# Attention and gated convolution on one core: x transposed by the DMA crossbar, exp written in token order, attention one step earlier

## The chip, the cores and the metric

The kernel runs on one core of a Trainium2 chip. The time is that of the device, in microseconds (us), from one launch; every kernel was timed several times on the same chip as the kernel before, in turn. A run counts as slow when it is more than 1.5% above the fastest of its kernel, and only fast runs enter a ratio. Engines are named as the profile has them: PE (TensorE matmul), PEld (weight load), DVE (VectorE), ACT (ScalarE), POOL (GpSimd), SP (SyncE, whose queue issues most stores and SBUF-to-SBUF transfers). PEclk is the TensorE clock that was granted, as a share of the full one.

## The reference, cut to what matters

Eight batches of eight heads, 576 tokens, head size 64. Keys and values are averaged over groups of eight tokens, so each head attends to 72 keys. The result x (576 x 512 a batch) goes through a feed-forward layer with a three-tap convolution along the tokens.

```
scores = q @ mean8(k).T / 8;  x = softmax(scores) @ mean8(v)      # per head
h   = relu(x @ w_in)                                              # 512 -> 1024
c   = conv_w[0]*h[t-1] + conv_w[1]*h[t] + conv_w[2]*h[t+1]        # along tokens
out = (h * sigmoid(c)) @ w_out                                    # 1024 -> 512
```

## The kernel before

One batch is 72 score columns a head on 72 partitions, then x with tokens on partitions, then xT with channels on partitions, because `mm1` contracts over channels. PSUM is four slots of two banks, shared by everything that PE writes; PE stops when no slot is free. A batch's loop has eight steps, each one `mm1` (eight matmuls) with a piece of the convolution, of `mm2` (an output tile) or of the next batch's attention between. Variable names: `sc_ps` scores, `attnT` their exp, `av_ps` attention times values, `h_ps` `mm1`, `c_ps` convolution, `o_ps` `mm2`, `kdup` the end of the key tree (three DVE additions that average the keys).

The scores of a head come out in the order (two, i, g), where token = 36 g + 2 i + two. Before, exp wrote rows of 16 adjacent elements in the kernel's own order, and the transpose of x put the tokens right without an instruction of its own, by a permuted identity and the copy out of PSUM:

```
def scores(b, h):
    ...                                         # two matmuls into ps[0:72, two, 0:288]
    nc.scalar.activation(
        out=at.rearrange("s (i two g) -> s two i g", two=2, g=QG),
        in_=ps[0:Sp, :, 0:SC].rearrange("s two (i g) -> s two i g", g=QG),
        func=ACT.Exp, scale=1.0 / (POOL * 8.0))

def xt(b, tiles):                               # PE transposes, 4 for each of 5 tiles
    ...
    nc.tensor.transpose(out=y[:, pr, :, ...], in_=st[b]["x"][i][...], identity=perm)
    ...
    nc.vector.tensor_copy(out=st[b]["xT"]...[:, :, :, r0:r0 + w - skip], in_=y[...])

def batch(b):                                   # cut: steps 4 to 7 of eight
    mm1(b, order[4]); conv(b, 0, 0); att[4](); pool_keys(b + 2); gate(b, 0, 0)
    mm1(b, order[5]); conv(b, 0, 1); att[5](); gate(b, 0, 1)     # att[5]: av 0, 1
    mm1(b, order[6]); tile_out(); ...; att[6](); att[7]()        # av 2-4; xt 0, 1
    mm1(b, order[7]); att[8](); tile_out()                       # xt 2-4
```

`pool_keys(n)` is the key tree of batch n, followed by the load of the keys of n + 1 into the buffer that the tree has just freed.

The softmax here doesn't subtract the row's maximum and nothing guards it: scores larger than these inputs give would overflow.

## Time and profile before

| | before |
|---|---|
| time, median of 3 runs | 250.67 us (248.53 to 253.44) |
| span of the profiled run | 245.7 us |
| steady batch (five loads of q, four intervals) | 26.5 us |
| PE transposes of x in a batch | 20, some 1.3 us of PE |
| exp | 64, 655 ns each |

The page of the profile of before. The first line is the busy time of each engine, with its share of the span and its instructions; the next two the chain of waits that ended last, by engine and by line; the others are groups of instructions (line, engine, operation, what it writes and reads, shapes, count | busy us, mean ns of one | idle time just before them and what ended it).

```profile
PE 218.3 (89%) x3153; PEld 142.7 (58%) x3153; DVE 156.9 (64%) x287; ACT 121.3 (49%) x209; POOL 30.9 (13%) x58
...
PE 62%; ACT 15%; DVE 11%; DMA 5%; issue 5%; POOL 0%; DVEq 0%; SPq 0%; ACTq 0%; POOLq 0%
PE o_ps L304 25%; PE h_ps L238 22%; ACT attnT L181 5%; PE q_ps L160 4%; PE c_ps L272 4%; ACT tg L281 4%; DVE x L205 3%; DVE o L314 3%; DMA qr<-in_q_dram 3%; DMA hT_108<-hT_108 3%; ACT hT_108 L246 3%; ACT hT_109 L246 2%; PE xt_ps L221 2%; PE kT_ps L148 1%; ACT o L312 1%
...
L238 PE MATMUL h_ps<-xT,w_in_sb 128*128 128x288 bf16 x512 | 77.3, 298 | 5.1 <-DVE xT L228 2.3
...
L181 ACT ACTIVATE attnT<-sc_ps 72x576 bf16<-72x576 f32 x64 | 37.2, 655 | 19.1 <-PE sc_ps L173 19.1
...
L221 PE MATMUL xt_ps<-perm,x 128*128 128x128 bf16 x160 | 15.1, 236 | 5.9 <-DVE x L205 3.9
```

PE is busy 89% of the span and makes up 62% of the chain. Exp takes 655 ns for 576 elements. The Trainium skill, "ScalarE: Activation LUTs", section "What ACT_TABLE_LOAD costs", gives 186 ns + 0.833 ns an element, which would be 666 ns: the trace agrees. The transposes' 15.1 us of PE are pipelined; eight of them move the chain by 0.52 us.

One line of before: the instructions that write the tile `perm` (count: least/median/most ns, first and last start).

```profile
L351 DVE COPY perm<-ident x1: 445/445/445, 6.0 to 6.0; 128x128 bf16<-128x128 bf16 x1
```

It is the only copy of before whose neighbouring writes lie far apart, 16 bytes here; memsets are left aside.

### The profile page before, as it was taken

How to read it: one execution, taken by the hardware profiler on the slowest of the kernel's cores; microseconds unless marked ns; L12 is line 12 of the kernel's file. 1: busy time of each engine (PE TensorE's matmuls, PEld its weight loads, DVE VectorE, ACT ScalarE, POOL GpSimd, SP SyncE). 2: the span in 40 equal slices, each digit the busy share in tenths (PEclk: the TensorE clock that was granted, in tenths of full speed). 3: DMA queues.
4: the chain of work that ended last, by engine and by line, in shares of the span. 5: the costliest groups of instructions: out<-in, count | busy, mean ns of one | idle time of the engine just before them, and what ended most of it. 6: DMA issues, size and time to landing. Idle time of an engine off the chain costs nothing.

```text
span 245.7 us, 7301 instructions
## 1 busy us (share of the span) xinstructions
PE 218.3 (89%) x3153; PEld 142.7 (58%) x3153; DVE 156.9 (64%) x287; ACT 121.3 (49%) x209; POOL 30.9 (13%) x58
## 2 busy tenths in 40 slices
PE   0487998559999999999999999999999999999993
PEld 0455665337666756666566665675666666656441
DVE  5678448683858585668684877668594826553341
ACT  2070379112681659236843586255925693267510
POOL 5442364010200011000200020001000000000000
PEclk9999999756999999999999999999999999999998
DMA  5999899969896288926895589628832223133323
GB/s 82 165 140 135 164 173 219 202 86 142 191 178 153 78 175 128 241 84 120 152 188 137 105 160 186 169 80 177 151 108 69 91 69 95 75 113 95 124 88 128
DMA packets 29908, 33.26 MB, mean 135 GB/s; under 512 B 5788, under 2 KB 24244, under 8 KB 29876
## 3 DMA queue, kind: packets, MB, share of 16 engines
q0 software_dynamic: 16976, 16.27, 45.0%
q1 hardware_dynamic: 12900, 16.54, 20.9%
q8 instruction: 24, 0.39, 0.6%
q14 instruction: 8, 0.07, 0.1%
HBM read 32.52 MB, written 9.44 MB: 171 GB/s over the span
## 4 chain that ended last, share of the span: by engine, by line
PE 62%; ACT 15%; DVE 11%; DMA 5%; issue 5%; POOL 0%; DVEq 0%; SPq 0%; ACTq 0%; POOLq 0%
PE o_ps L304 25%; PE h_ps L238 22%; ACT attnT L181 5%; PE q_ps L160 4%; PE c_ps L272 4%; ACT tg L281 4%; DVE x L205 3%; DVE o L314 3%; DMA qr<-in_q_dram 3%; DMA hT_108<-hT_108 3%; ACT hT_108 L246 3%; ACT hT_109 L246 2%; PE xt_ps L221 2%; PE kT_ps L148 1%; ACT o L312 1%
## 5 line engine op out<-in xcount | busy, mean ns | idle before, releaser
L238 PE MATMUL h_ps<-xT,w_in_sb 128*128 128x288 bf16 x512 | 77.3, 298 | 5.1 <-DVE xT L228 2.3
L304 PE MATMUL o_ps<-w_out_sb,gT 128*128 128x512 bf16 x288 | 67.1, 379 | 0.8 <-DVE gT L291 0.8
L238 PEld LDWEIGHTS <-w_in_sb 128*128 128x128 bf16 x512 | 50.6, 101 | 25.3 <-issue 7.9
L181 ACT ACTIVATE attnT<-sc_ps 72x576 bf16<-72x576 f32 x64 | 37.2, 655 | 19.1 <-PE sc_ps L173 19.1
L304 PEld LDWEIGHTS <-gT 128*128 128x128 bf16 x288 | 27.8, 98 | 29.5 <-DVE gT L291 1.3
L246 ACT ACTIVATE hT_109<-h_ps 128x576 bf16<-128x576 f32 x32 | 21.0, 656 | 44.5 <-PE h_ps L238 44.5
L281 ACT ACTIVATE tg<-c_ps 128x576 bf16<-128x576 f32 x64 | 38.4, 664 | 0.6 <-PE c_ps L272 0.6
L246 ACT ACTIVATE hT_108<-h_ps 128x576 bf16<-128x576 f32 x32 | 21.0, 657 | 24.9 <-PE h_ps L238 24.9
L205 DVE TENSOR_TENSOR x<-av_ps,r 128x512 bf16<-128x512 f32 x40 | 27.7, 692 | 1.4
L314 DVE COPY o<-o_ps 128x512 f32<-128x512 f32 x20 | 13.8, 692 | 18.2 <-PE o_ps L304 18.2
L312 ACT COPY o<-o_ps 128x512 f32<-128x512 f32 x16 | 9.4, 586 | 29.5 <-PE o_ps L304 29.5
L272 PEld LDWEIGHTS <-dw 32*32 32x32 bf16 x1536 | 14.1, 88 | 11.5 <-issue 8.0
L221 PE MATMUL xt_ps<-perm,x 128*128 128x128 bf16 x160 | 15.1, 236 | 5.9 <-DVE x L205 3.9
L221 PEld LDWEIGHTS <-x 128*128 128x128 bf16 x160 | 11.5, 104 | 8.6 <-DVE x L205 7.0
L194 PEld LDWEIGHTS <-attnT 72*128 72x128 bf16 x320 | 13.3, 102 | 4.3 <-ACT attnT L181 0.9
L113 POOL DMA_DIRECT2D qr<-in_q_dram x8 | 4.9, 617 | 81.9 <-PE q_ps L160 79.9
L165 DVE COPY qT<-q_ps 128x1152 bf16<-128x1152 bf16 x16 | 12.1, 756 | 4.8 <-PE q_ps L160 4.5
L173 PE MATMUL sc_ps<-qT,kz_104 128*72 128x288 bf16 x64 | 12.2, 326 | 1.2 <-DVE qT L165 0.8
L160 PE MATMUL q_ps<-ident,qr 128*128 128x128 bf16 x144 | 12.5, 243 | 0.7 <-DMA qr<-in_q_dram 0.7
L204 DVE RECIPROCAL r<-av_ps 128x8 f32<-128x8 f32 x40 | 8.0, 201 | 7.4 <-PE av_ps L194 7.4
L272 PE MATMUL c_ps<-hT_108,dw 32*32 32x288 bf16 x768 | 12.0, 287 | 0.8 <-ACT hT_108 L246 0.5
L228 DVE COPY xT<-xt_ps 128x1024 bf16<-128x1024 bf16 (+1 forms) x24 | 12.0, 548 | 0.1
(163 smaller groups left out, 188.8 us busy)
## 6 DMA issues: line engine op xcount, KB each, us to landing
out_dram<-o SPq DMA_DIRECT2D x36, 256.0 KB, 2.6
qr<-in_q_dram POOLq DMA_DIRECT2D x8, 576.0 KB, 6.2
kr<-in_k_dram POOLq DMA_DIRECT2D x7, 576.0 KB, 11.8
vr<-in_v_dram POOLq DMA_DIRECT2D x7, 576.0 KB, 10.8
hT_108<-hT_108 SPq DMA_DIRECT2D x16, 108.0 KB, 4.6
hT_109<-hT_109 SPq DMA_DIRECT2D x16, 108.0 KB, 4.0
hT_108<-hT_108 SPq DMA_DIRECT2D x16, 72.0 KB, 3.9
hT_109<-hT_109 SPq DMA_DIRECT2D x16, 72.0 KB, 2.2
```

What stands on the lines that cost most here:

```text
L160: nc.tensor.transpose(out=ps[:, i * P:(i + 1) * P], in_=st[b]["q"][:, i0 + i, :], identity=ident)
L173: nc.tensor.matmul(out=ps[0:Sp, c2, 0:SC], lhsT=kz[b % 2][:, h, c2, :], rhs=st[b]["qT"][:, h].rearrange("d i g -> d (i g)"), start=True, s ...
L181: nc.scalar.activation(out=at.rearrange("s (i two g) -> s two i g", two=2, g=QG), in_=ps[0:Sp, :, 0:SC].rearrange("s two (i g) -> s two i ...
L194: nc.tensor.matmul(out=ps[:, h // 4, c:c + D + 1], lhsT=st[b]["at"][h][:, t0:t0 + P], rhs=va[b % 2][:, h, :], start=True, stop=True,)
L205: nc.vector.tensor_tensor(out=x.rearrange("p (g h) d -> p g h d", g=2), in0=y[:, :, :, 0:D], in1=r.unsqueeze(3).to_broadcast([P, 2, 4, D]) ...
L221: nc.tensor.transpose(out=y[:, pr, :, ii * RT:(ii + 1) * RT], in_=st[b]["x"][i][:, 2 * pr:2 * pr + 2, :].rearrange("p h d -> p (h d)"), id ...
L238: nc.tensor.matmul(out=ps[:, c, 0:SC], lhsT=w_in_sb[:, dc, fb * P:(fb + 1) * P], rhs=xT[:, dc, c * SC:(c + 1) * SC], start=(dc == 0), stop ...
L246: nc.scalar.activation(out=row[:, PAD:S + PAD].rearrange("p (c n) -> p c n", c=NS), in_=ps[:, :, 0:SC], func=ACT.Relu, scale=0.5,)
L272: nc.tensor.matmul(out=ps[j // 2][QD * c:QD * (c + 1), j % 2, 0:SC], lhsT=dw[QD * r:QD * (r + 1), kk, g * NQ + j, :], rhs=row[QD * r:QD * ...
L281: nc.scalar.activation(out=tg[:, 2 * i:2 * i + 2, :], in_=ps[i][:, :, 0:SC], func=ACT.Tanh)
L304: nc.tensor.matmul(out=ps[:, 0, :], lhsT=gT[:, fb, j * P:(j + 1) * P], rhs=w_out_sb[:, fb, :], start=(fb == 0), stop=(fb == n_fb - 1),)
L314: nc.vector.tensor_copy(out=o, in_=ps[:, 0, :])
```

## The change

Its intent was to take the 140 transposes of batches 1 to 7 off PE and the copies off DVE. The crossbar transpose, as it is issued here, keeps the order of the tokens that it finds, so exp has to write them in token order. Attention moves up by a step to hide the transfers' time.

```diff
-            out=at.rearrange("s (i two g) -> s two i g", two=2, g=QG),
+            out=at.rearrange("s (g i two) -> s two i g", two=2, g=QG),
             in_=ps[0:Sp, :, 0:SC].rearrange("s two (i g) -> s two i g", g=QG),
...
+    def xt_dma(b, i):
+        t0, r0 = i * P, row0[i]
+        nc.sync.dma_start_transpose(
+            out=st[b]["xT"][:, :, t0:t0 + P - r0],
+            in_=st[b]["x"][i][r0:P].rearrange("p h d -> p (h d)"))
...   # xt() keeps PE for batch 0, now with the plain identity
         def a5():
-            av(n, 0)
-            av(n, 1)
+            for i in range(3):
+                av(n, i)
+                xt_dma(n, i)
         def a6():
...                                   # the same for tiles 3 and 4; a7, a8 gone
         mm1(b, order[0])
-        att[0]()
+        att[1]()                      # every att one step earlier
...
         mm1(b, order[4]); conv(b, 0, 0)
-        att[4](); pool_keys(b + 2); gate(b, 0, 0)
+        att[5](); gate(b, 0, 0); pool_keys(b + 2)
...
         mm1(b, order[7])
-        att[8]()
+        st[b + 2]["att"][0]()
         tile_out()
```

In exp only the output's layout changed: the innermost index g, adjacent before, now steps by 36 tokens, 72 bytes.

## The prediction

> **What bounds the kernel.** TensorE. The busy table gives PE 89% of the 245.7 us span, VectorE 64%, ScalarE 49%; the chain of waits is 62% PE, 15% ACT, 11% DVE. In the steady state one batch takes 25.7 or 27.1 us (four or five output tiles; read from the chain). Adding one batch's PE pieces from the chain (8 x 0.97 h_ps, 4.5 x 1.73 o_ps, 4 x 0.66 c_ps, 16 x 0.12 scores, 1.1 q, 0.4 k, 1.3 av, 1.3 xt) gives about 24.2 us, so some 2.2 us a batch are stalls, mostly where ScalarE's evictions (exp, tanh, Relu) free the four PSUM slots too late: the chain goes ACT attnT, hT, tg there.
>
> **Removed.** In seven batches 20 PE transposes each (8 took 0.52 us in the chain: 1.3 us a batch, 9 us in all, nearly all on the critical path), the three VectorE copies to xT (0.68+0.68+0.28 = 1.6 us a batch, mostly off it).
>
> **Added.** Five crossbar transposes a batch on SP's queue. SP now issues some 17 transfers a batch at 0.5-0.6 us. The Trainium skill, "VectorE: DVE Perf Modes", section "The three transpose paths", gives 1309 ns for one 128x128 by crossbar; no trace here shows one. My estimate: 1.2-2.5 us of SP per 128x512 transpose and about 3 us to land. The next batch's first mm1 needs the last two some 5 us after their issue: about covered, 0-1 us of stall a batch.
>
> **exp in token order.** Its innermost writes go from adjacent to 72 bytes apart. The Trainium skill, "Advanced Engine Details and Errata", section "SBUF Cachelines", says that a different 16-byte line for each access costs. The one such write in the trace agrees on VectorE: the perm copy (128 elements, 16 bytes apart) took 445 ns, where the fixed part of its copies is near 155 and one element a cycle would add 133. If ScalarE pays likewise (I say 60%), exp goes from 655 to about 1135 ns, 3.8 us a batch. In steps 1 to 3 (where tanh of two convs, Relu and eight exps now meet) ScalarE then has 14.7 us of work against 11.9 of PE, and PE loses about 2 us a batch there.
>
> **Moved.** Attention a step earlier puts av 0-2, two gates, the key tree (1.22+0.69+0.69), av 3-4, the kz and qT copies into steps 4 to 7: some 12 us of VectorE against 11 of PE. av 3 and 4 hold PSUM slots behind the key tree; I reckon 1.5-2.5 us of PE stall a batch there. That eats the 1.3 us.
>
> **Sum.** Without an exp penalty: about 246 us. With it: about 262 us (7 x 2 us, and some 2 us at the start). Weighted: 256 us, 8 in 10 between 240 and 272. Faster by over 2%: 0.28; within 2%: 0.22; slower: 0.5.
>
> **What would show it.** exp's mean in the groups of instructions (655 or over 1000 ns); the transposes' issue time on SP and their time to landing; in the waits, h_ps waiting for a DMA to xT (transposes late), PE waiting for x of VectorE (key tree in the way), or for attnT of ScalarE (exp slow); a steady batch of 25 us (right without penalty) or 27-28 us.
>
> **What would make it wrong.** ScalarE writing strided at full rate and VectorE keeping up: then 238-242. A transpose that keeps SP over 3 us: the queue then fills, hT turns and outputs come late, and it is over 270.

## The result

The changed kernel takes 363.5 us (median of 4 runs, 361.25 to 364.43) against 250.4 us for before (4 runs, 248.53 to 253.44). The ratio is 1.454, 95% interval 1.442 to 1.466. A ratio here is the mean time of one kernel's fast runs over that of the other's of the same rounds, so it is not quite the ratio of the medians quoted.

The page of the changed kernel, the same lines: busy time, chain, and the group of exp.

```profile
PE 244.8 (67%) x3013; PEld 148.2 (41%) x3013; DVE 145.7 (40%) x265; ACT 244.9 (68%) x209; POOL 30.3 (8%) x58
...
ACT 41%; PE 26%; DVE 12%; issue 10%; DMA 9%; POOL 0%; DVEq 0%; SPq 0%; ACTq 0%; POOLq 0%
ACT attnT L180 35%; PE h_ps L246 11%; PE o_ps L312 7%; DMA xT<-x 7%; DVE x L204 3%; PE c_ps L280 3%; PE q_ps L159 3%; ACT tg L289 2%; DMA qr<-in_q_dram 2%; DVE gT L299 2%; PE av_ps L193 2%; ACT hT_107 L254 1%; DVE r L203 1%; ACT hT_108 L254 1%; DVE kdup L135 1%
...
L180 ACT ACTIVATE attnT<-sc_ps 72x576 bf16<-72x576 f32 x64 | 163.2, 2883 | 11.1 <-PE sc_ps L172 11.1
```

One exp now takes 2883 ns in place of 655. (Records of exps that follow each other overlap. By busy time one exp costs 163.2 / 64 = 2.55 us of ACT against 37.2 / 64 = 0.58.) ACT's busy time has doubled, from 121 to 245 us, and it makes 41% of the chain, where PE had 62%. The list of waits (engine, line, what it waited for: us in total, times, longest) shows where PE lost its time.

```profile
PE sc_ps L172 <- ACT attnT L180: 41.1, 30, 2.1
...
PE av_ps L193 <- ACT attnT L180: 22.2, 12, 2.2
...
PE o_ps L312 <- ACT attnT L180: 11.5, 9, 1.5
...
PE h_ps L246 <- DMA xT<-x: 8.3, 4, 4.7
PE c_ps L280 <- ACT attnT L180: 7.4, 6, 1.6
```

These four waits of PE for exp add up to 82 us (41.1 + 22.2 + 11.5 + 7.4). The timeline shows how: in order of start, start and length in us, instructions merged, in brackets the idle time before.

```profile
182.08 1.12 PE L172 MATMUL sc_ps<-qT,kz_103 128*72 128x288 bf16 x4 [2.06 <-ACT attnT L180]
...
182.37 7.64 ACT L180 ACTIVATE attnT<-sc_ps 72x576 bf16<-72x576 f32 x3
...
187.59 0.40 PE L172 MATMUL sc_ps<-qT,kz_103 128*72 128x288 bf16 x2 [0.42 <-ACT attnT L180]
...
190.06 0.41 PE L172 MATMUL sc_ps<-qT,kz_103 128*72 128x288 bf16 x2 [2.07 <-ACT attnT L180]
```

Three exps take 7.64 us together, the next scores wait for a PSUM slot for up to 2.07 us, and so do convolution and output tiles, which use the same slots. The mean granted clock fell as well, to 0.849 (before 0.969); e12 below shows how a wait brings it down.

The crossbar did what was expected of it on SP's side. The tile xT in the trace (least/median/most ns of one issue; then us from issue to landing):

```profile
L216 SPq DMA_TRANSPOSE xT<-x x35: 1182/1218/2297, 72.7 to 326.8; - x35
...
DMA to landing us min/median/max: 2.3/3.1/7.9
```

A transpose of 128 x 512 elements keeps SP for 1.22 us and lands after 2.3 us at best.

### The profile page after: what moved, and what is told of

The parts are those of the page before. It is cut to its first block, busy times and chain, and to the rows that moved or that the text cites. A ratio compares the mean times of both kernels' runs of the same rounds, so it can differ in the third digit from the quotient of the medians.

```text
span 362.7 us, 7083 instructions
## 1 busy us (share of the span) xinstructions
PE 244.8 (67%) x3013; PEld 148.2 (41%) x3013; DVE 145.7 (40%) x265; ACT 244.9 (68%) x209; POOL 30.3 (8%) x58
## 4 chain that ended last, share of the span: by engine, by line
ACT 41%; PE 26%; DVE 12%; issue 10%; DMA 9%; POOL 0%; DVEq 0%; SPq 0%; ACTq 0%; POOLq 0%
ACT attnT L180 35%; PE h_ps L246 11%; PE o_ps L312 7%; DMA xT<-x 7%; DVE x L204 3%; PE c_ps L280 3%; PE q_ps L159 3%; ACT tg L289 2%; DMA qr<-in_q_dram 2%; DVE gT L299 2%; PE av_ps L193 2%; ACT hT_107 L254 1%; DVE r L203 1%; ACT hT_108 L254 1%; DVE kdup L135 1%
## 5 line engine op out<-in xcount | busy, mean ns | idle before, releaser
L180 ACT ACTIVATE attnT<-sc_ps 72x576 bf16<-72x576 f32 x64 | 163.2, 2883 | 11.1 <-PE sc_ps L172 11.1
L246 PE MATMUL h_ps<-xT,w_in_sb 128*128 128x288 bf16 x512 | 91.8, 334 | 9.7 <-DMA xT<-x 8.3
L312 PE MATMUL o_ps<-w_out_sb,gT 128*128 128x512 bf16 x288 | 71.0, 396 | 12.4 <-ACT attnT L180 11.5
L246 PEld LDWEIGHTS <-w_in_sb 128*128 128x128 bf16 x512 | 56.0, 112 | 36.3 <-DMA xT<-x 9.5
L254 ACT ACTIVATE hT_108<-h_ps 128x576 bf16<-128x576 f32 x32 | 23.9, 746 | 42.1 <-PE h_ps L246 42.1
L254 ACT ACTIVATE hT_107<-h_ps 128x576 bf16<-128x576 f32 x32 | 24.5, 767 | 33.8 <-PE h_ps L246 33.8
L193 PEld LDWEIGHTS <-attnT 72*128 72x128 bf16 x320 | 18.2, 123 | 27.1 <-issue 16.5
L172 PE MATMUL sc_ps<-qT,kz_104 128*72 128x288 bf16 x64 | 14.2, 321 | 22.1 <-ACT attnT L180 21.7
L172 PE MATMUL sc_ps<-qT,kz_103 128*72 128x288 bf16 x64 | 14.4, 341 | 20.6 <-ACT attnT L180 19.4
L280 PEld LDWEIGHTS <-dw 32*32 32x32 bf16 x1536 | 15.8, 91 | 24.5 <-issue 18.2
L193 PE MATMUL av_ps<-va_105,attnT 72*128 72x65 bf16 x160 | 10.5, 232 | 13.7 <-ACT attnT L180 13.5
L172 PEld LDWEIGHTS <-kz_104 128*72 128x72 bf16 x64 | 7.4, 121 | 28.9 <-issue 27.2
L172 PEld LDWEIGHTS <-kz_103 128*72 128x72 bf16 x64 | 8.3, 132 | 26.8 <-issue 22.8
L99 POOL DMA_DIRECT2D kr<-in_k_dram x9 | 7.3, 814 | 136.8 <-DVE t_840 L121 27.2
```

What stands on the lines that cost most here:

```text
L172: nc.tensor.matmul(out=ps[0:Sp, c2, 0:SC], lhsT=kz[b % 2][:, h, c2, :], rhs=st[b]["qT"][:, h].rearrange("d i g -> d (i g)"), start=True, s ...
L180: nc.scalar.activation(out=at.rearrange("s (g i two) -> s two i g", two=2, g=QG), in_=ps[0:Sp, :, 0:SC].rearrange("s two (i g) -> s two i ...
L193: nc.tensor.matmul(out=ps[:, h // 4, c:c + D + 1], lhsT=st[b]["at"][h][:, t0:t0 + P], rhs=va[b % 2][:, h, :], start=True, stop=True,)
L246: nc.tensor.matmul(out=ps[:, c, 0:SC], lhsT=w_in_sb[:, dc, fb * P:(fb + 1) * P], rhs=xT[:, dc, c * SC:(c + 1) * SC], start=(dc == 0), stop ...
L254: nc.scalar.activation(out=row[:, PAD:S + PAD].rearrange("p (c n) -> p c n", c=NS), in_=ps[:, :, 0:SC], func=ACT.Relu, scale=0.5,)
L280: nc.tensor.matmul(out=ps[j // 2][QD * c:QD * (c + 1), j % 2, 0:SC], lhsT=dw[QD * r:QD * (r + 1), kk, g * NQ + j, :], rhs=row[QD * r:QD * ...
```

## The experiments

There is no e10. Before ran too; its median is beside each result.

### Which part of the change costs the time: e1 to e4

**e1_exp_alone**: before, with exp's new write order and a plain identity in the PE transposes, nothing else.

```diff
-            out=at.rearrange("s (i two g) -> s two i g", two=2, g=QG),
+            out=at.rearrange("s (g i two) -> s two i g", two=2, g=QG),
```

> Before, with one part of the change: exp writes in token order (16 writes 72 bytes apart in a row), PE transposes with the plain identity, order of before. Theory W (the exp's write order costs nearly everything): exp near 2.9 us each, and 64 of them add some 143 us of ScalarE work, of which 90 to 120 us show: 340 to 370 us. Rival D (crossbar transposes or the moved attention slow the exp or cost the time): exp near 0.65 us, time within 10 us of before's 250.

372.3 us against 248.8, ratio 1.496, just above the range expected. The group of exp:

```profile
L182 ACT ACTIVATE attnT<-sc_ps 72x576 bf16<-72x576 f32 x64 | 163.9, 2894 | 18.6 <-PE sc_ps L174 18.6
```

Exp is as slow without a single crossbar transpose, and this kernel is slower than the whole change. Rival D falls: the write order alone costs more than the change loses, and the rest of the change wins a little back while ACT is the limit.

**e2_after_adjacent**: the changed kernel with the old, adjacent writes. The token order is then wrong.

```diff
-            out=at.rearrange("s (g i two) -> s two i g", two=2, g=QG),
+            out=at.rearrange("s (i two g) -> s two i g", two=2, g=QG),
```

> The changed kernel, with exp's writes adjacent again as before; crossbar transposes and moved attention stay. Wrong result on purpose (tokens in the kernel's inner order). Theory W: exp 0.65 us, time 240 to 256 us. Rival D: exp stays above 2 us or the time stays above 300 us.

265.8 us against 248.8, ratio 1.054; exp 649 ns. (Two of its four runs were slow; the fast ones took 261.5 and 263.2 us.) Most of the loss is gone, but not all: 265.8 lies between what the two theories said. With these small inputs the attention is nearly uniform; putting q's tokens into the wrong order in the reference itself changes the output by only 0.5% of its norm. So the comparison does not see token order here, and order has to be checked by reading.

**e3_after_i_inner** and **e4_after_two_inner**: the changed kernel, same elements, same places, same values; only the order in which the activation runs over them differs.

```diff
# e3: writes 4 bytes apart, PSUM read 64 bytes apart
-            out=at.rearrange("s (g i two) -> s two i g", two=2, g=QG),
-            in_=ps[0:Sp, :, 0:SC].rearrange("s two (i g) -> s two i g", g=QG),
+            out=at.rearrange("s (g i two) -> s two g i", two=2, g=QG),
+            in_=ps[0:Sp, :, 0:SC].rearrange("s two (i g) -> s two g i", g=QG),
# e4: writes adjacent, PSUM read alternating between two banks
+            out=at.rearrange("s (g i two) -> s g i two", two=2, g=QG),
+            in_=ps[0:Sp, :, 0:SC].rearrange("s two (i g) -> s g i two", g=QG),
```

> The changed kernel; exp computes and writes the same elements to the same places, but runs over i innermost: writes 4 bytes apart, PSUM reads 64 bytes apart. If the cost comes from the step between successive writes: exp 0.65 to 1.0 us, time as with adjacent writes, within 10 us. If it comes from the scattered layout as such, or from reading PSUM with a step as much as from writing: exp stays over 2 us.

> The same with two innermost: writes wholly adjacent, PSUM reads alternate between two banks (2048 bytes apart). If only the write step counts: exp 0.65 to 0.75 us and the fastest of the correct forms. If the read step counts too: slower than with i innermost.

e3 took 266.0 us (262.7 to 266.9, two of four runs slow) and e4 264.6 us, ratio 1.062; the times don't tell the two apart. The group of exp in e3 and in e4:

```profile
L180 ACT ACTIVATE attnT<-sc_ps 72x576 bf16<-72x576 f32 x64 | 45.7, 810 | 15.0 <-PE sc_ps L172 14.9
```

```profile
L180 ACT ACTIVATE attnT<-sc_ps 72x576 bf16<-72x576 f32 x64 | 37.0, 649 | 17.9 <-PE sc_ps L172 17.9
```

So the layout that the change wants costs exp nothing when the activation's innermost run is adjacent in SBUF. Neither of the two read patterns tried slowed it: with PSUM jumps of 2048 bytes between elements exp took 649 ns, and e3's 810 ns with PSUM steps of 64 bytes is what writes 4 bytes apart cost without them (806 ns, e11 below). The change's 363.5 us fall to e4's 264.6 us, 99 us, by an edit of the loop order.

**e5_order_pe**, a control: before with e4's exp order, the plain identity and PE transposes.

> Control: before with exp in token order by two innermost, plain identity, PE transposes, order of before. exp 0.65 us, time within 3 us of before: token order costs nothing when the innermost run is adjacent in SBUF.

250.5 us against 250.6; its profiled run was a slow one, and the ratio of the fast runs is 0.988, interval 0.977 to 0.999, from two fast runs. Token order is free in this kernel.

### How the cost grows with the step: e11

**e11_write_steps**: before with extra exps near the start, from one PSUM slot into a scratch tile, each form three times on its own line.

```diff
+    # k = 1, 2, 3, 4, 6, 8: one element every 2k bytes, never coming back
+    nc.scalar.activation(out=scr[...].rearrange("s (two n k) -> s two n k", two=2, k=k)[:, :, :, 0],
+                         in_=sps[0:Sp, :, 0:SC], func=ACT.Exp, scale=...)
+    # then the change's own form, i inner, two inner, and fp32 adjacent and 144 bytes apart
```

> Before with extra exps near the start into a scratch tile, three of each form: writes 2, 4, 6, 8, 12 and 16 bytes apart (monotone), the 72-byte interleaved form of the change, i innermost, two innermost, and fp32 adjacent and 144 bytes apart. If only the step between successive writes matters: 0.65 us up to some step, and as slow as 2.6 to 3.0 us at 16 bytes and above. If it is the coming back to the same lines that costs: 16 bytes monotone stays under 1.3 us and only the interleaved form is near 2.9.

The time (290 us) is that of before plus the extra work and says nothing. The groups of the scratch writes; L365 to L375 are steps of 2, 4, 6, 8, 12 and 16 bytes, L377 is the change's form, L379 i inner, L381 two inner, L383 fp32 adjacent, L385 fp32 144 bytes apart:

```profile
L375 ACT ACTIVATE scr<-sps 72x576 bf16<-72x576 f32 x3 | 8.1, 2710 | 0.1
...
L377 ACT ACTIVATE scr<-sps 72x576 bf16<-72x576 f32 x3 | 7.9, 2635 | 0.1
...
L373 ACT ACTIVATE scr<-sps 72x576 bf16<-72x576 f32 x3 | 6.2, 2075 | 0.1
...
L371 ACT ACTIVATE scr<-sps 72x576 bf16<-72x576 f32 x3 | 4.3, 1439 | 0.1
...
L385 ACT ACTIVATE scr<-sps 72x576 f32<-72x576 f32 x3 | 3.5, 1171 | 0.1
L369 ACT ACTIVATE scr<-sps 72x576 bf16<-72x576 f32 x3 | 3.4, 1122 | 0.1
...
L367 ACT ACTIVATE scr<-sps 72x576 bf16<-72x576 f32 x3 | 2.4, 806 | 0.1
L379 ACT ACTIVATE scr<-sps 72x576 bf16<-72x576 f32 x3 | 2.4, 804 | 0.1
L365 ACT ACTIVATE scr<-sps 72x576 bf16<-72x576 f32 x3 | 2.0, 650 | 0.1
L381 ACT ACTIVATE scr<-sps 72x576 bf16<-72x576 f32 x3 | 1.9, 647 | 0.1
L383 ACT ACTIVATE scr<-sps 72x576 f32<-72x576 f32 x3 | 1.9, 644 | 0.1
```

The times from 4 to 16 bytes lie on a line: 176 ns + 4.4 ns for each 16 bytes that the writes step through. A step of 4 bytes touches 144 such lines (estimate 810 ns, measured 806), 8 bytes 288 (1443; 1439), 12 bytes 432 (2077; 2075), 16 bytes 576 (2710; 2710). The two constants are fitted to these runs. At 72 bytes it is 2635 ns, no more than at 16, so the cost fits one charge for each 16-byte line entered, and it saturates. Coming back to the same lines (L377) is not what costs, as L375 never does. The Trainium skill, "Advanced Engine Details and Errata", section "SBUF Cachelines", names 16-byte lines and a penalty for a different line at each access; the trace agrees and adds the size. Four-byte elements pay less: 1171 ns at 144 bytes would be (1171 - 176) / 576 = 1.7 ns for each line, an estimate from this one point with the 176 ns of the two-byte line. Why two-byte writes pay 4.4 was not settled.

### What is left, 16 us: the crossbar or the move? e6 and e7

In e4 PE waited for xT and for the key tree:

```profile
PE h_ps L246 <- DMA xT<-x: 18.9, 6, 4.7
PE kT_ps L147 <- DVE kdup L135: 12.4, 3, 7.7
```

**e6_move_alone**: the earlier attention alone; exp, identity and PE transposes as before. The cut is shown against the changed kernel.

```diff
-            for i in range(3):
-                av(n, i)
-                xt_dma(n, i)
+            for i in range(3):
+                av(n, i)
...
+        att[7]()                      # xt 0, 1 by PE
         mm1(b, order[7])
+        att[8]()                      # xt 2 to 4 by PE
```

> The changed kernel's earlier attention alone: exp adjacent and PE transposes through perm, as before (transposes in the same place, end of the batch). Theory L (with exp mended, what is left of the loss is the crossbar transposes' latency at the end of a batch): 246 to 254 us, apart from the wait for kdup at the first handover (PE waited 7.7 to 9.4 us for it in the runs with exp mended), so up to 260. Rival M (the moved attention piles VectorE work up behind the key tree and costs the time): 258 us or more with PE waiting for x or kdup in every batch.

254.0 us against 250.8, ratio 1.011, interval 1.000 to 1.022. The move costs about 1%, and PE's longest listed waits (for `kdup`, 8.4 us) lie at two places only, not in every batch. Rival M falls.

**e7_crossbar_alone**: the crossbar, with e4's exp order, in the order of before.

```diff
         def a5():
             av(n, 0); av(n, 1)
+            xt_dma(n, 0); xt_dma(n, 1)
         def a6():
             av(n, 2); av(n, 3); av(n, 4)
+            xt_dma(n, 2); xt_dma(n, 3); xt_dma(n, 4)
-        def a7(): xt(n, [0, 1])
-        def a8(): xt(n, [2, 3]); xt(n, [4])
```

> Crossbar transposes alone, in the order of before, with exp in token order by two innermost (0.65 us). Theory L: av ends a step later than in the changed kernel, so the first matmuls of each batch wait longer for xT, 3 to 6 us more in each of seven batches: 275 to 300 us. Rival M: with the move undone the loss goes: 245 to 256 us.

276.0 us against 250.8, ratio 1.097. Its wait for xT:

```profile
PE h_ps L248 <- DMA xT<-x: 38.0, 12, 13.1
```

Twice e4's 18.9 us. The crossbar needs the move; with it, it still waits.

### Why the transposes land late: e8, e9, e12, e13, then e14

**e8_late_handover**: e4 with the second batch's key tree put back behind the first `mm1` of batch 1.

```diff
-        pool_keys(2)                  # end of the first batch
-        st[2]["att"][0]()
...
+        else:                         # batch 1, after mm1(b, order[0])
+            pool_keys(2)
+            att[0]()
```

> As e4_after_two_inner, but the second batch's key tree, its k turn and the first half of its q go back behind the first matmul group of batch 1, as before. If that early key tree only moves the wait for the load of k (PE waits for kdup 7.7 us at once): 256 to 262 us against e4's 264.6. If the wait for xT takes its place: no change, 263 to 266.

265.3 us, ratio 1.062, as e4. The wait for `kdup` fell from 12.4 to 6.3 us and that for xT rose from 18.9 to 25.2: the wait for xT took its place, as the second branch said.

**e9_mix**: e8, with tiles 3 and 4 by PE.

```diff
             for i in range(3, 5):
                 av(n, i)
-                xt_dma(n, i)
+        def a7():
+            xt(n, [3, 4])             # after mm1(b, order[7])
```

> As e8_late_handover, but only x tiles 0 to 2 go by crossbar; tiles 3 and 4, which are ready last, by PE. Theory L: the first half of mm1 needs tiles 0 to 2, issued 6 us earlier, so the waits for xT go, 12 of 20 transposes are saved (0.8 us a batch): 242 to 249 us, at or below before. Rival M: 256 us or more.

250.1 us against 250.8, ratio 1.000. The waits for xT went, apart from one of 5.2 us at the first handover, and so did the loss, but there was no gain: PE now waited 7.2 us for x.

**e12_keys_late** and **e13_mix_keys_late**: e8 and e9 with two edits more. Batch 1 is transposed by PE, and the key tree goes behind x tiles 3 and 4 in DVE's queue.

```diff
         att[5]()
         gate(b, 0, 0)
-        pool_keys(b + 2)
...
         att[6]()
         gate(b, 0, 1)
+        pool_keys(b + 2)
```

> Crossbar transposes of all five tiles for batches 2 to 7 (batches 0 and 1 by PE, as the loads crowd the DMA engines there), exp two innermost, and the key tree (2.6 us of VectorE) behind x tiles 3 and 4 instead of ahead of them. Theory L: tiles 3 and 4 are issued 2.6 us earlier, the waits for xT go, PE keeps the 1.3 us a batch: 240 to 247 us. If the last landing still comes too late (waits for xT of 1 us or more a batch): 248 to 256 us.

> The same, but tiles 3 and 4 by PE and only 0 to 2 by crossbar. Saves 0.8 us of PE a batch in six batches: 242 to 249 us, no wait for xT. If it is no faster than before, PE's stalls behind VectorE (x, o) took the saving.

e12 missed both its branches: 267.4 us against 250.6, ratio 1.064. e13: 250.7, ratio 0.992, interval 0.984 to 1.001, no clear gain. The edit hardly did what it was meant to do. At the handover below, x tiles 3 and 4 were ready at 103.4 and 104.2 us, but SP's queue held the first three transposes and two transfers of `hT` until 105.5 us. So the two went out 4.5 us ahead of the next batch's first matmul (105.99 against 110.51), where e8 had 4.1 us (113.78 against 117.89): 0.4 us gained in place of 2.6. So e12 does not test an earlier issue. Its timeline around that handover:

```profile
105.99 2.65 SPq L216 DMA_TRANSPOSE xT<-x  x2
...
106.80 0.80 POOL L99 DMA_DIRECT2D kr<-in_k_dram  x1 [15.32 <-DVE t L121]
...
110.51 0.65 PE L246 MATMUL h_ps<-xT,w_in_sb 128*128 128x288 bf16 x4
...
116.54 1.14 PE L246 MATMUL h_ps<-xT,w_in_sb 128*128 128x288 bf16 x4 [5.38 <-DMA xT<-x]
```

Two transposes are issued from 106.0 us. From 106.8 us POOL issues the load of the next keys, 576 KB, which the key tree has just made room for. The second half of `mm1` needs tiles 2 to 4 and waits 5.38 us, until 116.5. The same stretch by windows of 2 us (length, then busy us and instructions of PE, PEld, DVE, ACT and POOL, granted clock, DMA share, GB/s):

```profile
core 0: us, PE busy (x) PEld busy (x) DVE busy (x) ACT busy (x) POOL busy (x), PEclk, DMA share, GB/s
...
112.00:114.00 2.00, 0.00 (x0) 0.00 (x0) 0.00 (x0) 0.00 (x0) 0.00 (x0) 0.88 0.97 127
114.00:116.00 2.00, 0.00 (x0) 0.00 (x0) 0.00 (x0) 0.00 (x0) 0.00 (x0) 0.50 1.06 83
116.00:118.00 2.00, 1.46 (x36) 0.77 (x37) 0.00 (x0) 0.28 (x1) 0.00 (x0) 0.50 1.02 375
118.00:120.00 2.00, 2.00 (x60) 1.50 (x28) 0.30 (x1) 1.56 (x3) 0.04 (x1) 0.50 0.19 58
120.00:122.00 2.00, 2.00 (x58) 1.30 (x57) 1.97 (x4) 0.91 (x2) 0.55 (x1) 0.91 0.50 67
```

While PE waits, the DMA engines are fully taken (share about 1) at a mere 83 to 127 GB/s. The wait costs twice: the granted clock falls to 0.50 and is back at 0.91 only some four us after work returns. The Trainium skill, "TensorE: Matmul & The Clock Gate", section "Part 1: The HAM clock gate", has the clock halved after an idle window of about 3.4 us, which does not start with the idle time. The trace shows the half, but already some 2.4 us after PE went idle near 111.2 us (in windows of 0.5 us the clock is 1.00 until 113.5 us and 0.54 in the next), sooner than 3.4 us of idling alone would have it; at e12's next long wait, from 144.4 us, it came after some 3.3 us. For the slow transfers the Trainium skill, "DMA: Bandwidth & Descriptors", section "Issuing engines are not separate DMA queues", is the page to have in mind: transfers of all issuing engines run on the same 16 DMA engines and interleave. If so, that SP issues the transposes and POOL the load does not keep them apart; e14 tests it.

**e14_k_load_later**: e12, with the load of the keys moved behind the load of q in POOL's queue. The load of q waits for a PE transpose that comes after the batch's first `mm1`, so the keys now start when xT has arrived.

```diff
-            pool_keys(b + 2)          # key tree, then load_k(b + 3)
+            k_tree(b + 2, 0, H)
...
         att[1]()                      # first step: q, load_q(b + 2)
+        if b > 1 and b + 2 < B:
+            load_k(b + 2, 0, H)
```

> As e12_keys_late, but the next load of k is issued behind the load of q, after a batch's first matmuls, and no longer from the key tree just as transposes 3 and 4 go out. Theory C (what is left of the crossbar's loss is that its last transposes share the DMA engines with the k load): the worst landing falls from 9.0 to about 4 us, PE's waits for xT from 10.5 to under 4 us, time 244 to 254 us. Rival F (the crossbar's own latency is too long for this place): waits and time stay as in e12, 262 to 268 us.

250.0 us against 249.25, ratio 0.994, interval 0.988 to 1.001; e12 had 1.064. That is 17 us by moving one load. PE's list of waits has no wait for xT any more. The profiled runs show the double cost: of 18.6 us less span (263.8 to 245.2), 11.9 are idle time before `mm1` (15.9 to 4.0) and 5.7 are busy time of PE (215.2 to 209.5), whose matmuls had run at the halved clock. The landing times of e14:

```profile
DMA to landing us min/median/max: 2.3/2.9/6.4
```

For e12 and then for e16 below, which also has the moved load, the time that PE waited for xT, how often, and the landing times:

```profile
  DMA xT<-x: 10.5, 4
...
DMA to landing us min/median/max: 2.3/2.5/9.0
```

```profile
  DMA xT<-x: 1.8, 2
...
DMA to landing us min/median/max: 2.3/3.2/6.3
```

Theory C holds and rival F falls: the load is what makes the transposes late. That the two compete for the DMA engines, and not for another part that both use, is read from the engines' share of about 1 alone. The worst landing fell less than expected (to 6.4 us in e14), but the late ones no longer meet a waiting PE.

### A version that beats both, and what makes it: e15 to e18

**e15_mix_k_load_later**: e13 with the moved load.

> As e13_mix_keys_late (tiles 0 to 2 by crossbar, 3 and 4 by PE) with the k load moved the same way. Theory C: little to gain, as no wait for xT was left: 245 to 251 us. A candidate to beat before.

250.6 us, ratio 1.002: no gain from the mix.

**e16_k_load_later_keys_early**: e14 with the key tree ahead of tiles 3 and 4 again, as the change has it.

```diff
         att[5]()
         gate(b, 0, 0)
+        k_tree(b + 2, 0, H)
...
         gate(b, 0, 1)
-        k_tree(b + 2, 0, H)
```

> As e14, but the key tree ahead of x tiles 3 and 4 again, as in the change. Theory C: transposes 3 and 4 go out 2.6 us later, still without the k load beside them: slower than e14 by 0 to 7 us. If as fast: PE's position in the queue, not the key tree, set the end.

244.9 us against 249.25, ratio 0.985, interval 0.979 to 0.991: faster than both kernels, though by less than 2%. Its six runs (241.9 to 246.4 us) lie below the fastest of before (247.25). That it beats e5, the PE transposes with the new exp order (0.988, interval 0.977 to 0.999), is not shown. It is faster than e14, against what was expected of it. PE waited 11.9 us for `kdup` in e14, at seven places, and 6.0 us here, at three: a key tree that is late holds up the next batch's k transposes on PE.

**e17_pe_same_schedule**: e16 with all transposes by PE (the only edit is the set of tiles that go by crossbar, which is empty).

> Control of e16: the same schedule, exp order and k load, but every transpose by PE (at the end of the batch, behind the last matmul group). If e16's gain of 1.5% comes from the PE time that the crossbar saves: 248 to 253 us here. If it comes from the moved k load or the schedule: 242 to 246 us here as well.

252.9 us against 248.5, ratio 1.020, interval 1.014 to 1.026. So neither the moved load nor the schedule gives the gain; in the same schedule the crossbar is worth 3.5 points of ratio, 8 us of medians. Six batches at 1.3 us would be 7.8 us, the gain that the change was made for; e17 also has the copies to xT on DVE again. One reserve: e17 has all PE transposes at the very end of a batch, where e6 had some of them earlier, and e6 stood at 1.011; against that the crossbar is worth 2.6 points.

**e18_crossbar_from_batch_1**: e16 with batch 1 by crossbar too.

> As e16, but batch 1 goes by crossbar too, as in the change. Theory C: the start's loads crowd the DMA engines there (landings of 10 to 12 us in e4), so 3 to 9 us are lost at the handover to batch 1: 248 to 254 us. If it costs nothing: 243 to 246.

247.7 us against 248.5, ratio 0.996, interval 0.990 to 1.001: about 1% slower than e16, less than expected. Batch 1's wait for xT and its five landings, from a profiled run that was a slow one:

```profile
  DMA xT<-x: 11.7, 1
...
DMA to landing us min/median/max: 11.0/11.5/11.8
```

At the start, where the next q, k and v are still being loaded, no transpose landed in under 11 us.

## Why the prediction was wrong

It forecast 256 us, at most 272; the change takes 363.5.

- **The step that failed is the size of the exp penalty.** The prediction put it at "from 655 to about 1135 ns, 3.8 us a batch" and let PE lose "about 2 us a batch" to it. Measured: 2883 ns, and 126 us more busy time of ACT for the 64 exps (163.2 - 37.2), 15.8 us a batch; PE waited 82 us for exp, where the prediction had 16 in all. The mechanism (each write enters another 16-byte line) was right and was given a chance of 60%. The size came from DVE's perm copy, read as one more cycle an element, and carried over to ACT. Even that copy's own rate, (445 - 155) / 128 = 2.3 ns an element, would have given only about 1.5 us (175 ns + 576 x 2.3 ns, an estimate). ACT pays 4.4 ns for each line. ACT became the longest part of the chain (41%, before 15%), so little of it could hide: of the 126 us, 99 us show in the time (363.5 - 264.6).
- **"Without an exp penalty: about 246 us"** was wrong too; e4 takes 264.6. The prediction had the crossbar's waits at "0-1 us of stall a batch". PE waited 18.9 us for xT in the seven batches of e4 together, against at most 7 forecast, and the clock fell in the longer waits. The issue time (1.2 to 2.5 us forecast, 1.22 measured) and the landing in quiet (about 3 us forecast, 2.3 to 2.5 measured) were right. What was missing is the load of the next keys, which the key tree releases just then: e14 against e12 shows it.
- **The key tree in the way of av 3 and 4** ("1.5-2.5 us of PE stall a batch") was wrong. The move alone costs 1% (e6, where PE waited 3.2 us in all for x: 1.9 at `mm1`, 1.3 at the transposes), and putting the tree later made it slower (e14 against e16).
- **What bounds the kernel before and what the transposes are worth** was right as far as shown: 1.3 us of PE a batch agree with the 8 us between e17 and e16, under the reserve made there.
- The chances (0.5 for slower) leaned the right way. The range was too narrow since a cost known only from another engine was entered as if it were bounded at two cycles.

## What to carry to other kernels

Look at an engine's innermost write step in SBUF as at a cost of its own: put the strided side of a permuting instruction on the read from PSUM and let the innermost output run be adjacent; the same permutation then cost nothing here instead of 99 us. When work moves from an engine to the DMA queues, look for the loads that start in the same stretch, whoever issues them, and move those that have slack. Before trusting a comparison with the reference on element order, permute the reference and see whether it notices.

## What the Trainium skill lacked or had wrong

- "Advanced Engine Details and Errata", section "SBUF Cachelines", gives no size for the penalty. For bf16 writes of ACT it is 4.4 ns for each 16-byte line entered (806 ns at a step of 4 bytes, 2710 ns at 16, 2635 ns at 72, for 576 elements), for fp32 an estimated 1.7 ns (1171 ns at 144 bytes). It asks for at least two hits on a line to absorb the latency; two were not enough here: bf16 writes 8 bytes apart, two to a line, took 1439 ns against 650.
- "ScalarE: Activation LUTs", section "What ACT_TABLE_LOAD costs", gives 0.833 ns an element without a word on the access pattern. That held for adjacent writes (650 ns) and for PSUM reads 2048 bytes apart with adjacent writes (647 ns), not for strided writes.
- "VectorE: DVE Perf Modes", section "The three transpose paths", gives 1309 ns for a 128 x 128 crossbar transpose, without SP's issue time or the landing under load. A 128 x 512 transpose took 1.22 us of SP and 2.3 us to land at best, and up to 12.5 us beside loads (e4).
- "DMA: Bandwidth & Descriptors", section "Rules for kernel authors", says that a transpose next to ordinary DMAs needs nothing. That is about being right; for time, one ordinary load beside it was worth 17 us here (e12 against e14).
